# Two batches that share one pass over the weights: turns by quarters of ff in place of halves

## The chip, the cores and the metric

The kernel runs on one core of a Trainium2 chip. The metric is the device time of one execution, in microseconds (us). A core has TensorE (PE, matrix products into the accumulator memory PSUM), VectorE (DVE), ScalarE (ACT), GpSimd (POOL) and SyncE (SP). Each has its own instruction queue, which it works off in order; they wait for each other by semaphores. SP and POOL issue the transfers (DMA) of this kernel.

## The reference

```python
a = exp(phi - phi.max(axis=2)); a = a / (a.sum(axis=2) + 1e-9)   # phi: 8 batches, 8 heads, 576 tokens, 32 slots
k_m = einsum('bhsm,bhsd->bhmd', a, k)                            # k, v, q: 8, 8, 576, 64
v_m = einsum('bhsm,bhsd->bhmd', a, v)
attn = softmax(q @ k_m.T / 8, axis=-1)
x = (attn @ v_m) -> 4608 x 512
h = x @ w_in                                                     # 512 x 2048, float64 in memory
g = maximum(h, 0) ** 2
out = g @ w_out                                                  # 2048 x 512, float64 in memory
```

The weights arrive in float64 and leave as pairs of float32 numbers (a high and a low part); each product is made of three products of such parts.

## The kernel before, in words

**Pairs of batches.** The 8 batches are worked in pairs. One batch is 576 tokens: 512 main rows in four groups of 128, and 64 leftover rows, which are kept until both batches of a pair can put theirs together into one group of 128. The hidden width ff = 2048 is cut into 16 blocks of 128; two blocks make a slice (8 slices).

**A step** (`step(g)`) is one batch and one ff block. `mm1` makes 12 matmuls into two PSUM tiles (tile `h`), ScalarE and VectorE turn them into the high and low part of the squares (tiles `gh`, `glo`, lines 609 to 613; for the leftover rows tile `gl`, lines 610 and 614), and `mm2` makes 12 matmuls that add this block's share of the output into four PSUM accumulators (`acc`, lines 633 to 636). The list `seq` says which batch and block each step is. As long as successive steps belong to one batch, the accumulators go on; where the batch changes, they are evacuated (`evac`) to on-chip memory and the other batch takes them over. `mm2_left` makes the product of the leftover rows of a pair, 48 matmuls into a fifth accumulator that shares the same four places (tile `accl`, line 659).

**The first pair decodes the weights.** `piece(kind, j)` decodes slice j of w_in or w_out in two halves (`decode`, lines 320 to 346): a load of float64 bits into a raw room (SP), six or seven VectorE operations and two ScalarE operations in a work room, and, for w_out after the first slice, a transfer on POOL that adds the work room to the low part (line 343, `wo<-work`). The decoded w_in (tile `wi`, three places) is stored to memory as two float32 parts (POOL, line 346) and read again by `wi_again` (SP, line 351) whenever another batch needs it; the decoded w_out (tiles `wo`) stays on chip. The rooms are tiles that are not yet in use: `free` lists them for each slice, V4 to V7 (later holders of products and of partial sums), the W tiles of later slices, and for slice 7 the tiles of q and of keys and values (`KV`).

**Products with the values.** `memory(b, hh)` makes the attention memory of half of a batch's heads (products `pkv`, line 408, from tiles `KV` and `phi`); `vw_alone` (pair 0) and `vw_step` (later pairs) multiply the slices of w_in by the values' memory, so that the attention's output x is never formed. `attention(b)` makes the attention weights of a batch (tiles `ath`, `atl`; the last subtraction is line 570); its tile q is loaded by line 515.

**Order.** The program lists operations with what they read and write. `Plan.order` lays them on the engines by a list schedule: each operation has a latest start that follows from the due time of its step, `due(g) = (g + 20) * 5200` ns, and from the estimated costs of what comes behind it; of what is ready, an engine takes the operation with the earliest latest start, where preparing operations (`lead`) count 9000 ns earlier. So an operation's place on its engine follows from the position of its step in `seq`. In the first pair `seq` has batch 0 with blocks 0 to 7, batch 1 with 0 to 15, and batch 0 with 8 to 15: 32 steps, numbered 0 to 31. The attention of batch 1 is needed from step 8 on, and slices 4 to 7 at steps 16, 18, 20 and 22.

Of the kernel before, what the change touches and what calls it, by code (L numbers as in the profile page):

```python
# [11 lines left out]
F32 = mybir.dt.float32  # L12
# [7 lines left out]
P = 128  # L20
# [186 lines left out]
def tile_attention_moe(  # L207
# [79 lines left out]
    half = NFF // 2  # L287
    seq = [(b, f) for b, h in ((0, 0), (1, 0), (1, 1), (0, 1)) for f in range(h * half, (h + 1) * half)]
    seq += [(b, f) for b in range(2, B) for f in range(NFF)]
# [292 lines left out]
    def mm1(g):  # L582
# [7 lines left out]
        if ff not in gl or gl[ff][0] != b // 2:  # L590
            gl[ff] = b // 2, st([P, 2, 2 * LEFT], F32R, f"gl{ff}", f"gl{g}")
        G = gl[ff][1]
        lc = slice((b % 2) * LEFT, (b % 2 + 1) * LEFT)
        for h in (0, 1):
# [15 lines left out]
        op({"ACT": act(LEFT)}, lambda e: nc.scalar.activation(G()[:, 0, lc], r()[:, SM:S], AF.Square), [r], [(G, (b % 2, 0))])  # L610
# [3 lines left out]
        vec({"DVE": tt(LEFT)}, lambda e: nc.vector.tensor_sub(G()[:, 1, lc], r()[:, SM:S], G()[:, 0, lc].bitcast(F32)), [r, (G, (b % 2, 0))], [(G, (b % 2, 1))])  # L614
        gt[g] = gh, glo

    def mm2(g):
# [21 lines left out]
        if f1:  # L639
            home = homes(b) if ff == NFF - 1 else None  # L640
            for i in range(NMAIN):
                if ff < NFF - 1:
                    if i % 2 == 0:
                        part[i // 2] = st([P, 2, DM], F32, f"V{4 + i // 2}", f"part{i // 2}")
                    pp = part[i // 2]
                    op({"ACT": act(DM), "DVE": tt(DM)}, lambda e, i=i, a=acc[i], pp=pp: copy(e, pp()[:, i % 2, :], a()), [acc[i]], [(pp, i % 2)])
                else:
                    ot, x = home[i]
                    evac(acc[i], home[i], lambda ot=ot, x=x: ot()[:, x, :], [(b, 4 * i + c) for c in range(4)], b == 0)

    def mm2_left(b, g):
        a = pt("acc", f"accl{b}", 4)
        for ff in range(NFF):
            G = gl[ff][1]
            t = wo[ff]

            def mm(e, ff=ff, G=G, t=t):
                for n, (l, w) in enumerate(((0, 0), (0, 1), (1, 0))):
                    nc.tensor.matmul(a(), G()[:, l, :], t()[:, w],  # L659
                                     start=(ff == 0 and n == 0), stop=(ff == NFF - 1 and n == 2))  # L660

            op({"PE": 690}, mm, [G, (t, 0), (t, 1)], [a], cap=due(g + 2) + 690 * ff, lat=300)
        o = st([P, DM], F32, "o", f"ol{b}")
        evac(a, (o, None), lambda: o(), [(b - 1, 16), (b - 1, 17), (b, 16), (b, 17)])

    def homes(b):

        if b == 0:
            return [(part[i // 2], i % 2) for i in range(NMAIN)]
        tags = ("V6", "V7") if b == 1 else ("vw0", "vw0") if b % 2 == 0 else ("V4", "V5")  # L670
# [3 lines left out]
    def evac(a, home, o, cols, add=False):  # L674
        if add:
            vec({"DVE": tt(DM)}, lambda e: nc.vector.tensor_add(o(), a(), o()), [a, home], [home], port=None)
        else:
            op({"ACT": act(DM), "DVE": tt(DM)}, lambda e: copy(e, o(), a()), [a], [home])
        n = len(cols) // len({x[0] for x in cols})
        for j in range(0, 4, n):  # L680
            b, c = cols[j]

            def store(d, j=j, b=b, c=c):
# [3 lines left out]
            dma(store, 32 * n * DM * 4, [home], [], eng="SP" if b >= B - 2 else "POOL")  # L687


    pos = {x: i for i, x in enumerate(seq)}  # L690

    def step(g):
# [3 lines left out]
        if ff == NFF - 1 and b % 2 == (b > 1):  # L696
            mm2_left(b | 1, g)
# [3 lines left out]
        0: ("V6 V7 W6a", "W6b W7a W7b V4 V5"), 4: ("V6 V7 W5a", "W5b W6a W6b W7a W7b"),  # L701
        5: ("V6 V7", "W6a W6b W7a W7b"), 6: ("V6 V7", "W7a W7b"), 7: ("V6 V7", "q KV"),
# [3 lines left out]
    def piece(kind, j):  # L706
        raws, works = (x.split() for x in free[j if j > 3 else 0])
# [9 lines left out]
    for j in range(4):  # L717
# [9 lines left out]
    for s in range(4):  # L727
        vw_alloc(0, s, (1,))
        for hh in (0, 1):
            wi_again(0, s, hh)  # L730
        vw_alone(s, 1)
        step(8 + 2 * s)
        step(9 + 2 * s)
    for j in range(4, 8):
# [5 lines left out]
        step(8 + 2 * j)  # L740
        step(9 + 2 * j)
    for g in range(24, 32):
        step(g)
# [50 lines left out]
```

## Time and profile before

| | |
|---|---|
| median of 3 runs (all) | 836.11 us (831.14, 836.11, 837.33) |
| span of the profiled execution | 831.4 us; the page gives no time around it |
| TensorE busy | 763.5 us, 92% |
| VectorE busy | 571.2 us, 69% |
| ScalarE busy | 378.1 us, 45% |
| GpSimd busy | 67.4 us, 8% |
| granted TensorE clock, mean | 0.973 |
| moved by transfers | 101.56 MB, mean 122 GB/s |

The profile is one execution. Busy times of an engine are the union of its instructions' times; instructions that are pipelined overlap, so durations of single instructions add up to more than the busy time. The granted clock is a share of full speed: 1.0 is 2.4 GHz, 0.5 is 1.2 GHz, and a value between is a mean over a stretch with both. "Idle before, releaser" is the time in which an engine had nothing running before an instruction, and what let it go on.

### The profile page before, as it was taken

What the parts mean: (1) busy time and instruction counts of PE and PEld (TensorE: products, weight loads), DVE (VectorE), ACT (ScalarE), POOL (GpSimd) and SP (SyncE); (2) the same over time, 40 slices, a digit from 0 to 9 for tenths busy, and PEclk for the clock granted to TensorE, in tenths of its full rate; (3) what the DMA queues carried; (4) which work ended last, traced back from release to release, by engine and by line L of the source; (5) the groups of instructions that cost most, each with busy time, mean ns of one, the idle gap of its engine ahead of it and who ended that gap; (6) DMA issues with size and microseconds to landing.
All of it is one profiled execution on the core that took longest, in us unless ns stands there. A gap on an engine that the chain in (4) does not pass through costs nothing.

```text
span 831.4 us, 12939 instructions
## 1 busy us (share of the span) xinstructions
PE 763.5 (92%) x4756; PEld 643.3 (77%) x4756; DVE 571.2 (69%) x1266; ACT 378.1 (45%) x871; POOL 67.4 (8%) x105
## 2 busy tenths in 40 slices
PE   3468789989989899999999999999999999999995
PEld 2245578878768688888888888888788888888884
DVE  3899899898446756696768465786768556774540
ACT  1235466656535245563436355463435355552320
POOL 3113112222100100001000100000000100000000
PEclk9959999999999899999999999999999999999998
DMA  7947966657665443322552533323422433100001
GB/s 210 302 153 223 261 192 203 178 174 212 159 161 151 116 132 102 102 80 52 143 142 72 135 111 99 117 54 81 140 61 69 138 93 99 53 16 36 1 1 63
DMA packets 93091, 101.56 MB, mean 122 GB/s; under 512 B 24868, under 2 KB 78116, under 8 KB 93028
## 3 DMA queue, kind: packets, MB, share of 16 engines
q1 hardware_dynamic: 80292, 81.55, 33.2%
q0 software_dynamic: 12736, 19.19, 9.5%
q8 instruction: 37, 0.61, 0.3%
q14 instruction: 26, 0.21, 0.1%
HBM read 79.17 MB, written 17.83 MB: 117 GB/s over the span
## 4 chain that ended last, share of the span: by engine, by line
PE 73%; issue 10%; DVE 8%; DMA 3%; ACT 2%; POOL 2%; SPq 0%; POOLq 0%; DVEq 0%; ACTq 0%
PE h L603 20%; PE acc L636 12%; PE acc L633 12%; PE acc L634 12%; PE accl L659 4%; PE pvw L494 4%; PE psc L532 3%; PE pkv L408 3%; DMA q<-in_q_dram 2%; PE pvw L475 1%; DVE vw L503 1%; DVE qT L527 1%; ACT vw L260 1%; DMA wo<-work 1%; DVE work L325 1%
## 5 line engine op out<-in xcount | busy, mean ns | idle before, releaser
L603 PE MATMUL h<-ath,vw 128*128 128x320 f32 (+1 forms) x1024 | 213.9, 300 | 8.9 <-ACT ath L260 6.3
L633 PE MATMUL acc<-wo,gh 128*128 128x512 f32 x512 | 207.0, 404 | 2.7 <-ACT gh L609 2.5
L634 PE MATMUL acc<-wo,gh 128*128 128x512 f32 x512 | 201.7, 394 | 0.0
L603 PEld LDWEIGHTS h<-ath,vw 128*128 128x128 f32 x1024 | 172.5, 190 | 25.7 <-ACT ath L260 6.7
L636 PE MATMUL acc<-wo,glo 128*128 128x512 f32 x512 | 161.5, 409 | 3.0 <-DVE glo L613 2.8
L503 DVE TENSOR_TENSOR vw<-pvw,vw 64x256 fp32r<-64x256 f32 x192 | 78.5, 420 | 68.0 <-ACT vw L260 66.2
L633 PEld LDWEIGHTS acc<-wo,gh 128*128 128x128 f32 x512 | 97.1, 190 | 23.3 <-ACT gh L609 3.8
L260 ACT CAST vw<-pvw 64x256 fp32r<-64x256 f32 (+1 forms) x206 | 74.9, 381 | 83.9 <-PE pvw L494 37.6
L603 PE MATMUL h<-atl,vw 128*128 128x256 f32 (+1 forms) x512 | 110.5, 297 | 0.0
L634 PEld LDWEIGHTS acc<-wo,gh 128*128 128x128 f32 x512 | 96.9, 189 | 16.9
L636 PEld LDWEIGHTS acc<-wo,glo 128*128 128x128 f32 x512 | 90.5, 191 | 21.4 <-DVE glo L613 7.6
L609 ACT ACTIVATE gh<-r 128x512 fp32r<-128x512 f32 x128 | 80.7, 631 | 45.3 <-DVE r L608 38.5
L613 DVE TENSOR_TENSOR glo<-r,gh 128x512 fp32r<-128x512 f32 x128 | 87.6, 684 | 5.1 <-ACT r L611 2.9
L608 DVE TENSOR_SCALAR r<-h 128x256 f32<-128x256 f32 (+1 forms) x109 | 49.7, 458 | 59.0 <-PE h L603 58.1
L607 ACT ACTIVATE r<-h 128x256 f32<-128x256 f32 (+1 forms) x147 | 58.8, 407 | 67.8 <-PE h L603 59.8
L603 PEld LDWEIGHTS h<-atl,vw 128*128 128x128 f32 x512 | 83.0, 190 | 0.5 <-DVE atl L570 0.2
L611 ACT ACTIVATE r<-r 128x576 f32<-128x576 f32 x93 | 63.7, 685 | 2.1
L610 ACT ACTIVATE gl<-r 128x64 fp32r<-128x64 f32 x128 | 32.7, 256 | 63.2 <-DVE r L608 61.0
L659 PE MATMUL accl<-wo,gl 128*128 128x512 f32 x192 | 53.0, 400 | 0.1
L532 PE MATMUL psc<-qT,kb 128*128 128x256 f32 (+1 forms) x128 | 43.3, 465 | 5.8 <-DVE S L536 3.1
L494 PE MATMUL pvw<-wi,VTh 128*128 128x256 f32 x192 | 38.1, 290 | 3.8 <-DVE vw L503 3.7
L659 PEld LDWEIGHTS accl<-wo,gl 128*128 128x128 f32 x192 | 35.4, 191 | 7.3 <-DVE o L260 0.5
(94 smaller groups left out, 818.5 us busy)
## 6 DMA issues: line engine op xcount, KB each, us to landing
wi<-w_in_hi SPq DMA_DIRECT2D x56, 256.0 KB
wi<-w_in_lo SPq DMA_DIRECT2D x56, 256.0 KB
q<-in_q_dram SPq DMA_DIRECT2D x32, 288.0 KB
KV<-in_k_dram SPq DMA_DIRECT2D x32, 256.0 KB
KV<-in_v_dram SPq DMA_DIRECT2D x32, 256.0 KB
raw<-in_moe_w_in_dram SPq DMA_DIRECT2D x16, 512.0 KB
raw<-in_moe_w_out_dram SPq DMA_DIRECT2D x16, 512.0 KB
out_dram<-o POOLq DMA_DIRECT2D x20, 256.0 KB, 8.4
```

Source lines behind the costliest of these rows:

```text
L260: nc.scalar.copy(o, i) if e == "ACT" else ENG[e].tensor_copy(o, i)
L494: nc.tensor.matmul(pw()[:, x * SL:(x + 1) * SL], l()[:, 2 * hh + x, :], w(r, x), start=(i == 0), stop=(i == 2))
L503: vec({"DVE": tt(SL)}, lambda e, V=V, pr=pr, src=src: nc.vector.tensor_sub(V()[pr, 1, hh, :], src(), V()[pr, 0, hh, :].bitcast(F32)), [pw, ...
L532: nc.tensor.matmul(pq()[:, 0:32 * n], kb()[:, x].rearrange("p h m -> p (h m)"), qT()[:, x, 0:n].rearrange("p c t -> p (c t)"), start=(x == ...
L603: nc.tensor.matmul(p()[:, 0:n], V()[:, l, hh, c0:c0 + P], x()[:, hh, cs], start=(i == 0), stop=(i == 5))
L609: op({"ACT": act(SM)}, lambda e: nc.scalar.activation(gh(), r()[:, 0:SM], AF.Square), [r], [gh])
L611: op({"ACT": act(S), **({} if b < 2 else {"DVE": tt(S)})}, lambda e: nc.scalar.activation(r(), r(), AF.Square) if e == "ACT" else nc.vecto ...
L613: vec({"DVE": tt(SM)}, lambda e: nc.vector.tensor_sub(glo(), r()[:, 0:SM], gh().bitcast(F32)), [r, gh], [glo])
L633: nc.tensor.matmul(a(), gh()[:, c], t()[:, 0], start=f0, stop=False)
L634: nc.tensor.matmul(a(), gh()[:, c], t()[:, 1], start=False, stop=False)
L636: nc.tensor.matmul(a(), glo()[:, c], t()[:, 0], start=False, stop=f1)
L659: nc.tensor.matmul(a(), G()[:, l, :], t()[:, w], start=(ff == 0 and n == 0), stop=(ff == NFF - 1 and n == 2))
```

## The change

The first pair's turns become quarters of ff, and neighbouring turns of one batch are joined: batch 0 with blocks 0 to 3, batch 1 with 0 to 7, batch 0 with 4 to 11, batch 1 with 8 to 15, batch 0 with 12 to 15. Every time a batch hands the accumulators over, its sums go to its four places on chip (V4, V5 for batch 0; V6, V7 for batch 1): the first time as a copy, later by an addition that only VectorE may do; the last time they are stored too. The leftover rows' squares are kept by quarters (four tiles `gl0` to `gl3`, of which the first pair uses two), and their product is made in four parts as soon as both batches have a quarter. The decoder's rooms and the tiles of the products move accordingly.

```diff
+    turns = [(b, range(4 * x, 4 * x + 4)) for x in range(4) for b in ((0, 1) if x % 2 == 0 else (1, 0))]
+    turns += [(b, range(NFF)) for b in range(2, B)]
+    joined = [turns[0]]
+    for b, fs in turns[1:]:
+        if b == joined[-1][0]:
+            joined[-1] = b, range(joined[-1][1].start, fs.stop)
+        else:
+            joined.append((b, fs))
+    seq = [(b, f) for b, fs in joined for f in fs]
...
-            later = 0 if n == 0 and s > 3 else 1
+            later = 1 if n or s // 2 % 2 == 0 else 0
...
-        ts_ = [wi[0, s, bp if s < 4 else 0, hh] for hh in (0, 1)]
+        ts_ = [wi[0, s, bp if s < 2 else 0, hh] for hh in (0, 1)]
...
+            new = b not in part
+            if new:
+                part[b] = homes(b)
             for i in range(NMAIN):
...
+                ot, x = part[b][i]
+                o = lambda ot=ot, x=x: ot()[:, x, :]
+                evac(acc[i], (ot, x), o, not new)
+                if ff == NFF - 1:
+                    store((ot, x), o, [(b, 4 * i + c) for c in range(4)])
...
-    def mm2_left(b, g):
+    def mm2_left(b, g, fs):
...
+        last = {}
+        for x in (b - b % 2, b - b % 2 + 1):
+            last[x] = max((f for bb, f in seq[:g + 1] if bb == x), default=-1) + 1
+        stop = min(last.values())
+        start = done.get(b // 2, 0)
+        if stop > start:
+            mm2_left(b | 1, g, range(start, stop))
+            done[b // 2] = stop
...
-        0: ("V6 V7 W6a", "W6b W7a W7b V4 V5"), 4: ("V6 V7 W5a", "W5b W6a W6b W7a W7b"),
-        5: ("V6 V7", "W6a W6b W7a W7b"), 6: ("V6 V7", "W7a W7b"), 7: ("V6 V7", "q KV"),
+        0: ("V6 V7 W6a", "W6b W7a W7b V4 V5"), 2: ("V6 V7 W6a", "W6b W7a W7b"), 4: ("W6a W7a W5a", "W6b W7b W5b"),
+        5: ("W6a W7a gl2", "W6b W7b gl3"), 6: ("W7a gl2", "W7b gl3"), 7: ("gl2 KV", "gl3 q"),
...
-    for j in range(4):
+    for j in (0, 1):
         piece("wi", j)
         vw_alloc(0, j, (0,))
         vw_alone(j, 0)
...
-    for s in range(4):
-        vw_alloc(0, s, (1,))
...
-    for j in range(4, 8):
+    g = 4
+    for j in range(NSL):
+        if j < 2:
+            vw_alloc(0, j, (1,))
+            for hh in (0, 1):
+                wi_again(0, j, hh)
+            vw_alone(j, 1)
+            for _ in (0, 1):
+                step(g)
+                g += 1
+            continue
         piece("wi", j)
         vw_alloc(0, j)
         for bp in (0, 1):
             vw_alone(j, bp)
         piece("wo", j)
...
```

In `free` the first list of a slice are the raw rooms and the second the work rooms. `memory(1, ...)` and `attention(1)` stand ahead of the second loop in both kernels; before, four slices stand ahead of them, after, two. `mm2_left` takes the blocks of one part as `fs`, evacuates the first part by a copy and the later ones by additions. `wi_again` runs for four slices of the first pair before and for two after.

## Rows read from the trace of the kernel before

**Rows 1.** The page's picture of the span in 40 slices: TensorE busy, TensorE clock, tenths.

```profile
PE   3468789989989899999999999999999999999995
PEclk9959999999999899999999999999999999999998
```

**Rows 2.** Stages: length, busy us of PE, PEld, DVE, ACT, POOL; clock, transfer share, GB/s.

```profile
62.00:97.00 35.00, 27.39 (x191) 20.95 (x191) 31.18 (x72) 15.90 (x36) 8.01 (x11) 0.90 0.86 241
97.00:125.00 28.00, 23.29 (x124) 18.70 (x124) 27.90 (x64) 16.77 (x38) 4.72 (x6) 1.00 0.69 204
125.00:208.00 83.00, 78.53 (x473) 69.82 (x471) 72.96 (x146) 51.31 (x111) 19.04 (x24) 1.00 0.66 192
208.00:270.00 62.00, 57.54 (x435) 46.33 (x433) 33.87 (x79) 29.32 (x70) 3.61 (x8) 0.97 0.61 158
270.00:291.00 21.00, 17.57 (x74) 14.54 (x74) 16.06 (x35) 5.44 (x14) 2.68 (x4) 0.84 0.46 115
291.00:420.00 129.00, 128.85 (x827) 111.19 (x826) 90.39 (x205) 64.90 (x154) 4.64 (x9) 1.00 0.36 100
```

**Rows 3.** Order of time of VectorE, 62 to 290 us: start, length, line, operation.

```profile
70.78 0.68 DVE L339 TENSOR_TENSOR wo<-work,wo 128x512 fp32r<-128x512 f32 x1
104.38 0.69 DVE L613 TENSOR_TENSOR glo<-r,gh 128x512 fp32r<-128x512 f32 x1
112.87 0.68 DVE L339 TENSOR_TENSOR wo<-work,wo 128x512 fp32r<-128x512 f32 x1
124.08 0.49 DVE L570 TENSOR_TENSOR atl<-at,ath 128x320 fp32r<-128x320 f32 x1
125.42 0.69 DVE L613 TENSOR_TENSOR glo<-r,gh 128x512 fp32r<-128x512 f32 x1
201.67 0.68 DVE L339 TENSOR_TENSOR wo<-work,wo 128x512 fp32r<-128x512 f32 x1
266.65 0.69 DVE L613 TENSOR_TENSOR glo<-r,gh 128x512 fp32r<-128x512 f32 x1
281.66 0.71 DVE L527 STREAM_TRANSPOSE qT<-q 128x512 f32<-128x512 f32 x1 [3.33 <-DMA q<-in_q_dram]
```

**Rows 4.** Groups of VectorE, 125 to 208 us: count, busy us, mean ns, idle before.

```profile
L327 DVE SCALAR_TENSOR_TENSOR work<-raw,work 128x512 f32<-128x512 uint32 x16 | 10.9, 684 | 0.1
L324 DVE TENSOR_SCALAR work<-raw 128x512 uint32<-128x512 uint32 x15 | 6.5, 432 | 0.0
L322 DVE TENSOR_SCALAR work<-raw 128x512 f32<-128x512 f32 x13 | 5.5, 422 | 4.9 <-DMA wo<-work 3.1 <-DMA raw<-in_moe_w_in_dram 1.6 <-DMA raw<-in_moe_w_out_dram 0.2
```

**Rows 5.** Instructions on the tile part: count, ns least/median/most, first and last start.

```profile
L676 DVE TENSOR_TENSOR part<-acc,part x4: 668/682/692, 270.5 to 285.5; 128x512 f32<-128x512 f32 x4
L260 ACT COPY part<-acc x3: 582/587/592, 128.1 to 130.2; 128x512 f32<-128x512 f32 x3
L260 DVE COPY part<-acc x1: 682/682/682, 130.5 to 130.5; 128x512 f32<-128x512 f32 x1
```

**Rows 6.** Order of time of TensorE where batch 1 hands over to batch 0.

```profile
224.04 0.63 PE L636 MATMUL acc<-wo,glo 128*128 128x512 f32 x2
226.16 0.39 PE L633 MATMUL acc<-wo,gh 128*128 128x512 f32 x1
```

**Rows 7.** Transfers issued from 0 to 210 us: line, count, size.

```profile
wi<-w_in_hi SPq DMA_DIRECT2D x11, 256.0 KB
```

**Rows 8.** Order of time of TensorE before batch 2's first product.

```profile
214.93 1.43 PE L408 MATMUL pkv<-KV,phi 128*32 128x128 f32 x38
254.87 1.43 PE L408 MATMUL pkv<-KV,phi 128*32 128x128 f32 x40
286.99 0.63 PE L603 MATMUL h<-ath,vw 128*128 128x256 f32 x2
```

**Rows 9.** Order of time of the queues of POOL and SP after slice 7.

```profile
202.65 0.85 POOL L343 DMA_DIRECT2D wo<-work  x1 [4.84 <-DVE wo L339]
203.03 0.37 SPq L359 DMA_DIRECT2D KV<-in_k_dram  x1
```

More of the change, by code (lines that the diff above doesn't have):

```diff
@@ L639, in mm2 @@
         if f1:
-            home = homes(b) if ff == NFF - 1 else None
+            new = b not in part
+            if new:
+                part[b] = homes(b)
             for i in range(NMAIN):
[L642 to L649, printed above, removed]
-    def mm2_left(b, g):
-        a = pt("acc", f"accl{b}", 4)
-        for ff in range(NFF):
-            G = gl[ff][1]
+                ot, x = part[b][i]
[4 more added lines that the diff above has]
+    def mm2_left(b, g, fs):
+        a = pt("acc", f"accl{b}_{fs.start}", 4)
+        for ff in fs:
+            G = gl[b // 2, ff // 4]
             t = wo[ff]
@@ L658, in mm, with evac @@
                 for n, (l, w) in enumerate(((0, 0), (0, 1), (1, 0))):
[L659 to L664, printed above, removed]
+                    nc.tensor.matmul(a(), G()[:, ff % 4, l, :], t()[:, w],
+                                     start=(ff == fs.start and n == 0), stop=(ff == fs.stop - 1 and n == 2))
+            op({"PE": 690}, mm, [(G, (ff % 4, x, l)) for x in (0, 1) for l in (0, 1)] + [(t, 0), (t, 1)], [a], cap=due(g + 2) + 690 * ff, lat=300)
+        if fs.start == 0:
+            part["left"] = st([P, DM], F32, "o", f"ol{b}")
+        o = part["left"]
+        evac(a, (o, None), lambda: o(), fs.start > 0)
+        if fs.stop == NFF:
+            store((o, None), lambda: o(), [(b - 1, 16), (b - 1, 17), (b, 16), (b, 17)])
     def homes(b):
-        if b == 0:
-            return [(part[i // 2], i % 2) for i in range(NMAIN)]
-        tags = ("V6", "V7") if b == 1 else ("vw0", "vw0") if b % 2 == 0 else ("V4", "V5")
+        tags = ("V4", "V5") if b == 0 else ("V6", "V7") if b == 1 else ("vw0", "vw0") if b % 2 == 0 else ("V4", "V5")
         t = [st([P, 2, DM], F32, x, f"o{b}_{i}", 2 if x == "vw0" else 1) for i, x in enumerate(tags)]
         return [(t[i // 2], i % 2) for i in range(NMAIN)]
-    def evac(a, home, o, cols, add=False):
+    def evac(a, home, o, add):
         if add:
@@ L681, in evac, with st_ @@
             b, c = cols[j]
-            def store(d, j=j, b=b, c=c):
+            def st_(d, j=j, b=b, c=c):
                 rows = out[b * S:(b + 1) * S, :].rearrange("(p c) e -> c p e", c=NC)
                 d(rows[c:c + n], o()[32 * j:32 * (j + n), :])
-            dma(store, 32 * n * DM * 4, [home], [], eng="SP" if b >= B - 2 else "POOL")
+            dma(st_, 32 * n * DM * 4, [home], [], eng="SP" if b >= B - 2 else "POOL")
     pos = {x: i for i, x in enumerate(seq)}
+    done = {}
     def step(g):
@@ L706, in piece @@
     def piece(kind, j):
-        raws, works = (x.split() for x in free[j if j > 3 else 0])
+        raws, works = (x.split() for x in free[max(x for x in free if x <= j)])
         for h in (0, 1):
@@ L739, in tile_attention_moe @@
         piece("wo", j)
[L740 to L743, printed above, removed]
+        for _ in (0, 1):
+            step(g)
+            g += 1
+        if j % 2:
+            for _ in range(4):
+                step(g)
+                g += 1
     for n in range(1, NPAIR):
```

25 lines of the change are left out of this document (10 added, 15 removed).

## The prediction

> **What bounds the kernel now.** I read the page's picture of the span first, then the busy time of each engine by stage, then VectorE's order of time in the opening, then the way in which the second pair of batches starts.
>
> The picture [rows 1] shows TensorE busy in nine tenths of nearly every slice from 125 us on, and not before; its clock line has its lows in the same opening and once more near 280 us. The stages [rows 2] give sizes. From 62 to 97 us TensorE is idle for 35.00 - 27.39 = 7.6 us, from 97 to 125 for 4.7, from 125 to 208 for 4.5, from 208 to 270 for 4.5 and from 270 to 291 for 3.4: together 24.7 us. After 291 us it idles 0.15 us in 129, so nothing there can be won by order. What holds TensorE in the opening is VectorE: 31.18 of 35 us and 27.90 of 28 us busy. From 125 to 208 VectorE is still at 88%, and from 208 to 270 at 55%: the bound passes to TensorE at about 125 us.
>
> VectorE's order of time [rows 3] says what the opening waits for. The weights of slices 0 and 1 (each slice is 256 columns of ff, two steps) are decoded at 70.78 + 0.68 = 71.5 us. The fourth step's subtraction is at 104.38, slice 3 is decoded at 113.6, the attention of batch 1 ends at 124.6, and the eighth step's subtraction is at 125.42. From there the 24 further steps of the pair take until 266.65: 141.2 / 24 = 5.9 us a step. So up to 125 us a step waits for the decoder, and batch 1, which needs no new weights for its first eight steps, cannot help, because its attention is only finished when the first eight steps are done.
>
> **The change part by part.** All sums are against the profiled execution, of which the page gives the span, 831.4 us, and no time around it. The runs are 831.14, 836.11 and 837.33 us: the span lies 4.7 us under their median and 0.3 over the lowest. I take differences from the trace and put them on the median.
>
> *The order of steps.* Steps 0 to 3 stay batch 0, 4 to 11 become batch 1, 12 to 19 batch 0, 20 to 27 batch 1, 28 to 31 batch 0. Due times follow the position, so the attention of batch 1 is due four steps earlier, slices 2 and 3 four steps later, slices 4 and 5 as before, slices 6 and 7 four steps later (26 in place of 22 for slice 7). What VectorE has to do before step 4 is now: both attentions and two slices, in place of one attention, three slices. Price of a slice: a half of w_in takes three VectorE operations of the short kind and four of the long one, a half of w_out (slices after the first) three and three, so a slice is 12 x 0.43 + 14 x 0.68 = 14.7 us by durations [rows 4], and by start distances, which are 0.08 us shorter each, 12.6. Between 71.5 and 125 us VectorE did two slices (25.2), eight subtractions (4.8), three products' splits (1.8), the idle 35 - 31.18 + 0.1 = 3.9 us at most, and, for the beginning of slice 4 and the small parts, some 4 us more by estimate; what is left, about 14 us, was attention of batch 1. If that 14 us comes first, behind four subtractions (2.4), four splits (2.4) and the same waits, it ends at 71.5 + 14 + 4.8 + 3.9 = 94 us, in place of 124.6. From 94 us TensorE has eight steps without new weights; at 5.9 us each the eighth subtraction falls at 94 + 4 x 5.9 = 117.6 in place of 125.42. Slice 2 is then due at step 8 and ready at 94 + 12.6 + 3 = 110, slice 3 at step 10 (129 us) and ready at 126: in time, barely. Gain 7.8 us. Its bounds: 12.3 us, all idle time of 62 to 125, and -5.9, one step lost because attention now comes ahead of slice 1. I take **7**, the nearest whole value, since the order of steps is what these rows show.
>
> *From 125 to 208 us* slices 6 and 7 are due four steps later, so TensorE should wait less for them. Idle there is 4.5 us; bounds 0 and 4.5, taken **2**, the middle.
>
> *Evacuations.* Four accumulators change owner five times in place of three, and the left product ends four times in place of once: 13 evacuations become 24, and all 11 more are additions, which only VectorE may do, at 0.68 us [rows 5]: 7.5 us of VectorE. Today's copies go three to ScalarE and one to VectorE. Where they change owner at step 23 TensorE ends the old step at 224.04 + 0.63 and starts the new at 226.16, with the next products of the first layer between [rows 6]: no wait. Four additions in a row need 2.7 us of VectorE alone, where the cover is one step's first product, so two more changes may cost 0 to 2 x 2.7 us; I take **-1**, nearer to the row that shows no wait. The left products themselves are the same 48 matmuls a pair: nothing. The additions lie where VectorE is 55 to 88% busy; if that cover were gone they would cost their 7.5 us (a rival, below).
>
> *Queues.* On SP the re-reads of w_in for batch 1 fall from 16 to 8 transfers of 256 KB in the first pair; the row counts 11 of each half up to 210 us, of which 8 are this pair's [rows 7]. That is 2.1 MB less, at the 204 GB/s of 97 to 125 us 10 us of the transfers' time, in a stage where TensorE does not wait for them: no gain counted. On POOL the stores of w_in and the adding transfers of w_out keep their number and order; batch 1's stores move four steps later and stand behind the last adding transfers, so nothing waits for them. The decoder's work rooms fall from five to three for slices 2 to 4, its raw rooms stay three; VectorE lost 3.1 us to an adding transfer with five and four rooms [rows 4], so I set 0 to 5 us of VectorE waits, hidden up to step 8's reserve; none counted.
>
> *Where it can be given back.* Batch 2's first product starts at 286.99 [rows 8]. It stands behind the keys and values of batches 2 and 3, whose first load waits for slice 7's last adding transfer: issued at 202.65, load at 203.03 [rows 9], and then products of memory at 214.93, ..., 254.87: 13.3 us each, paced by loads. From load to first product are 84 us. After the change, slice 7 ends about 2 us later by VectorE's count: seven of the eleven additions fall ahead of it (4.8 us), less some of the 4.9 us of waits [rows 4]. The 32 us from 254.87 to 286.99 can shrink: VectorE is 55% busy there and waits 3.33 us for q [rows 3]. I estimate 9 us of shrinking, so 287 + 2 - 9 = 280. TensorE's side gives 287 - 7 - 2 + 1 = 279. The later of both holds: batch 2 starts at 280, **7 us earlier**, and from there the kernel is TensorE's and unchanged. 836.1 - 7 = **829**.
>
> **The rivals.**
> *All of it is kept (822).* Idle of 62 to 125 falls from 12.3 to 3, of 125 to 208 from 4.5 to 1.5, and the start of batch 2 loses 2.9 of its 7.9 us, since loads that are asked for earlier meet fewer re-reads: 9.3 + 3 + 2.9 - 1 = 14 us. For it: transfers are 86% busy in 62 to 97, and 2.1 MB of them go. Against: the 13.3 us rounds.
> *The 84 us stand (838).* The opening gains 7 us, or the planner leaves the order of engines nearly as it was, and batch 2 still waits 84 us for the load, which comes 2 us later: +2. For it: those rounds. Against: 32 us of the chain are not loads.
> *Slice 7 slides (851).* It is due four steps later and holds two rooms of keys and of q until its last adding transfer. Placed by its due time at today's pace it ends 23.5 us later; the load is at 226.5, and with the shortened 75 us batch 2 starts at 301.5, 14.5 us late. It decides from a load at 220.4 on, where the start passes 295.4. For it: VectorE serves what is due first. Against: VectorE has idle time, and the same rooms are due to batch 2 as well.
> *VectorE is the bound throughout (844).* Then 11 additions cost their 7.5 us. Rows speak against it: VectorE is full to 125 us alone, and at most two of the eleven fall there. The Trainium skill, Perfetto Trace Analysis, section Identifying the Most-Contended Engine, names the engine with the highest occupancy as the one to relieve first; by that the opening would be VectorE's, and a change that gives it more work would lose. The trace agrees for the opening and not for the stages in which the additions lie.
>
> **How the numbers follow.** The forecast has 0.42 (own range 824 to 834), all kept 0.28, the 84 us 0.13, the slide 0.10, VectorE 0.07. A measurement of this kernel can tell about 1%, 8.4 us, from no change: under 827.7 or over 844.5. Faster: 0.27 of all kept and 0.06 of the forecast, 0.33. Slower: the slide, 0.10, and 0.04 of the upper ends of the others, 0.14. The rest, 0.53, is within. The range reaches from 818, beyond all kept, to 844, at VectorE's; outside lie the slide and the far end of all kept, under 0.2.
>
> **What would show it.** The attention of batch 1 ending near 94 us and the eighth subtraction near 118 show the first step right; an end past 110 shows it wrong. Idle of TensorE from 62 to 125 should be about 5 us. The last adding transfer of slice 7 near 205 and batch 2's first product near 280 show the handing over right; a load after 220 is the slide. TensorE waiting for additions at steps 12, 20 and 28 would show my -1 too small. A VectorE that is full after 125 us would prove the last rival.

## The result and the profile after

| | before | after |
|---|---|---|
| median | 834.63 us (4 runs, 831.14 to 837.33) | 824.41 us (4 runs, 821.78 to 826.54) |
| ratio after / before, 95% interval | | 0.9879 [0.9839, 0.9919] |
| profiled execution: span | 831.4 us | 823.8 us (its time 825.51) |
| TensorE, VectorE busy | 763.5, 571.2 us | 762.6, 576.0 us |
| moved by transfers | 101.56 MB | 99.46 MB |

The change makes the kernel 10.2 us faster, 1.2%. In the profiled executions the span is 7.6 us shorter; TensorE's busy time differs by 0.9 us, so 6.7 us of it are idle time that is gone. The question of this section is where.

The page's picture of the changed kernel, in 40 slices, for [rows 1]:

```profile
PE   3358889999999999999999999999999999999995
PEclk9977989999999999999999999999999999999998
```

The low places that the kernel before has from 166 to 291 us (single 8s in the busy line, an 8 in the clock line near 280 us) are gone. The opening, the first five or six digits, looks no better. The stages of the changed kernel say it in numbers (length, busy us of PE, PEld, DVE, ACT, POOL, then clock, transfer share, GB/s), for [rows 2]:

```profile
62.00:97.00 35.00, 29.22 (x192) 22.14 (x193) 26.91 (x60) 14.93 (x35) 4.94 (x7) 0.83 0.73 223
97.00:125.00 28.00, 24.07 (x119) 19.77 (x118) 24.73 (x55) 16.22 (x37) 5.04 (x6) 0.88 0.43 127
125.00:208.00 83.00, 81.46 (x473) 71.44 (x472) 80.39 (x165) 54.98 (x117) 21.29 (x26) 1.00 0.64 181
208.00:270.00 62.00, 59.15 (x449) 47.96 (x448) 45.05 (x103) 26.37 (x64) 6.84 (x12) 1.00 0.68 185
270.00:291.00 21.00, 21.00 (x117) 18.13 (x116) 19.40 (x43) 13.33 (x34) 4.01 (x6) 1.00 0.56 134
291.00:420.00 129.00, 128.84 (x867) 111.12 (x866) 91.45 (x205) 65.85 (x156) 3.29 (x7) 1.00 0.38 106
```

Length less busy time of TensorE, against [rows 2]: 62 to 97 us 5.8 (before 7.6), 97 to 125 us 3.9 (4.7), 125 to 208 us 1.5 (4.5), 208 to 270 us 2.9 (4.5), 270 to 291 us 0.0 (3.4). Before 62 us the changed kernel idles 3.4 us more than the kernel before, so the whole opening, 0 to 125 us, went from 44.4 to 45.2: nothing was won there. From 125 to 291 us idle time fell from 12.4 to 4.4, by 8.0 us; after 291 us it rose by 0.5. The three together are the 6.7 us.

The clock's lows in this stretch are gone too. The granted clock is 1.00 in all three stages from 125 us on, where the kernel before had 1.00, 0.97 and 0.84: there it was 0.50, which is 1.2 GHz, from 243.6 to 246.8 us, after TensorE had waited 3.00 us until 242.00, and again from 288 to 291 us, after a wait of 3.43 us until 285.57. What the slower clock cost by itself is not separated here.

VectorE's order of time of the changed kernel (start, length, line, operation, in brackets the idle time before it and what ended it), for [rows 3]; lines have moved, L621 is the subtraction `glo`, L345 the last operation of a half slice, L576 the last of an attention:

```profile
82.47 0.68 DVE L621 TENSOR_TENSOR glo<-r,gh 128x512 fp32r<-128x512 f32 x1
94.69 0.52 DVE L542 STREAM_TRANSPOSE S<-psc 128x320 f32<-128x320 f32 x1 [3.71 <-PE psc L538]
107.75 0.49 DVE L576 TENSOR_TENSOR atl<-at,ath 128x320 fp32r<-128x320 f32 x1
134.62 0.68 DVE L621 TENSOR_TENSOR glo<-r,gh 128x512 fp32r<-128x512 f32 x1
218.62 0.69 DVE L345 TENSOR_TENSOR wo<-work,wo 128x512 fp32r<-128x512 f32 x1
280.33 0.65 DVE L621 TENSOR_TENSOR glo<-r,gh 128x512 fp32r<-128x512 f32 x1
```

The attention of batch 1 does move ahead, from 124.6 to 108.2 us, but by 16 us and not by 30; the eighth subtraction falls at 134.62, 9 us later than before. VectorE, full before (59.1 us busy of 63 from 62 to 125 us), now idles 11.4 of them: 3.71 us of it in one piece behind TensorE's scores. Two more pauses of 2.4 us each stand behind TensorE's products for `vw` and for the memory. An attention is a chain that goes to and fro between TensorE, VectorE and ScalarE, and with the decoder's slices placed after it VectorE has less to fill its pauses with. Slice 7 ends at 218.62 + 0.69 in place of 202.4 us, and the pair's last subtraction falls at 280.33 in place of 266.65: the first pair now runs further into the stretch in which the second is made ready.

Batch 2's keys and values and its first product, TensorE's order of time in the changed kernel, for [rows 8]:

```profile
209.28 1.43 PE L414 MATMUL pkv<-KV,phi 128*32 128x128 f32 x38
246.07 1.54 PE L414 MATMUL pkv<-KV,phi 128*32 128x128 f32 x40 [0.25 <-DMA KV<-in_v_dram]
282.07 0.40 PE L611 MATMUL h<-ath,vw 128*128 128x256 f32 x2
```

And the two queues, POOL's and SP's, in the changed kernel, for [rows 9]:

```profile
213.81 0.91 POOL L349 DMA_DIRECT2D wo<-work  x1 [1.51 <-DVE wo L345]
219.60 0.84 POOL L349 DMA_DIRECT2D wo<-work  x1 [4.88 <-DMA KV<-in_v_dram]
...
203.50 0.37 SPq L365 DMA_DIRECT2D KV<-in_k_dram  x1
218.86 1.14 SPq L521 DMA_DIRECT2D q<-in_q_dram  x2
```

In the kernel before, SP waited 7.6 us for an adding transfer until it could issue the load at 203.03. That was not the last one, which was issued at 202.65, only 0.38 us ahead, but the one before it:

```profile
196.89 0.92 POOL L343 DMA_DIRECT2D wo<-work  x1 [0.82 <-DVE gl L614]
SPq L359 <- DMA wo<-work: 7.6, 1, 7.6
```

By the semaphores in the trace this transfer, issued at 196.89, landed at 202.90 and let the load of keys go; the last one landed at 207.41 and let the load of q go at 207.54. In the changed kernel the last two adding transfers slid to 213.81 and 219.60 us, the load of keys only to 203.50: it no longer stands behind either, but behind VectorE's last read of the room (L333). The load of q at 218.86 still stands behind an adding transfer, the one of 213.81. Products of memory run 6 to 9 us earlier, and batch 2 starts at 282.07 in place of 286.99.

In the decoder, VectorE's groups of the changed kernel from 125 to 208 us (count, busy us, mean ns, idle before) answer to [rows 4]:

```profile
L333 DVE SCALAR_TENSOR_TENSOR work<-raw,work 128x512 f32<-128x512 uint32 x19 | 12.9, 680 | 0.0
L328 DVE TENSOR_SCALAR work<-raw 128x512 f32<-128x512 f32 x17 | 7.6, 446 | 1.2 <-DMA wo<-work 1.2
```

VectorE waits 1.2 us there for work rooms in place of 3.1, no longer waits for raw loads (1.8 us before), and is busy for 80.39 us of 83 in place of 72.96. The evacuations, for [rows 5] (the tile is now called `o`; instructions on it by VectorE from 100 to 300 us, ns least/median/most, first and last start):

```profile
L685 DVE TENSOR_TENSOR o<-acc,o x12: 645/691/692, 204.6 to 286.1; 128x512 f32<-128x512 f32 x12
L260 DVE COPY o<-acc x2: 676/678/679, 155.0 to 155.6; 128x512 f32<-128x512 f32 x2
```

TensorE's waits from 125 to 291 us in the changed kernel (us, times, longest):

```profile
PE psc L538 <- DVE rz_None L555: 1.6, 1, 1.6
PE h L611 <- ACT r L615: 1.3, 1, 1.3
PE pvt L451 <- DVE vx L447: 1.0, 2, 0.8
PE accl L666 <- DVE o L685: 0.5, 1, 0.5
PE accl L666 <- DVE o L260: 0.5, 1, 0.5
PE pvw L481 <- DVE vw L489: 0.4, 1, 0.4
PE pkv L414 <- DMA KV<-in_v_dram: 0.2, 1, 0.2
```

Before, the longest in the same view were the splits `vw` (VectorE late) and the keys and values:

```profile
PE pvw L494 <- DVE vw L503: 3.4, 1, 3.4
PE pkv L408 <- DMA KV<-in_v_dram: 3.0, 1, 3.0
PE pvw L475 <- DVE vw L483: 2.5, 2, 2.2
```

These 8.9 us are now 0.6. That is about the gain; the experiments ask what took them away.

### The profile page after: what moved, and what is told of

The parts are those of the page before. It is cut to its first block, busy times and chain, and to the rows that moved or that the text cites. A ratio compares the mean times of both kernels' runs of the same rounds, so it can differ in the third digit from the quotient of the medians.

```text
span 823.8 us, 12916 instructions
## 1 busy us (share of the span) xinstructions
PE 762.6 (93%) x4756; PEld 643.3 (78%) x4756; DVE 576.0 (70%) x1276; ACT 378.3 (46%) x872; POOL 67.8 (8%) x105
## 2 busy tenths in 40 slices
DMA packets 90915, 99.46 MB, mean 121 GB/s; under 512 B 24740, under 2 KB 75940, under 8 KB 90852
## 4 chain that ended last, share of the span: by engine, by line
PE 74%; DVE 9%; issue 8%; ACT 3%; DMA 3%; POOL 1%; SPq 0%; POOLq 0%; DVEq 0%; ACTq 0%
PE h L611 20%; PE acc L641 13%; PE acc L642 12%; PE acc L644 12%; PE accl L666 5%; PE pvw L500 4%; PE psc L538 3%; PE pkv L414 3%; DMA phi<-in_phi_dram 1%; PE pvw L481 1%; DMA q<-in_q_dram 1%; ACT vw L260 1%; DVE glo L621 1%; DVE work L331 1%; DVE work L333 1%
## 5 line engine op out<-in xcount | busy, mean ns | idle before, releaser
L509 DVE TENSOR_TENSOR vw<-pvw,vw 64x256 fp32r<-64x256 f32 x192 | 78.6, 420 | 63.9 <-ACT vw L260 62.0
L615 ACT ACTIVATE r<-h 128x320 f32<-128x320 f32 (+1 forms) x148 | 59.4, 407 | 85.5 <-PE h L611 79.3
L616 DVE TENSOR_SCALAR r<-h 128x320 f32<-128x320 f32 (+1 forms) x108 | 49.2, 457 | 59.7 <-PE h L611 59.0
L621 DVE TENSOR_TENSOR glo<-r,gh 128x512 fp32r<-128x512 f32 x128 | 87.4, 683 | 4.9 <-ACT r L619 3.1
L538 PE MATMUL psc<-qT,kb 128*128 128x256 f32 (+1 forms) x128 | 41.4, 448 | 5.4 <-DVE S L542 1.8
L696 POOL DMA_DIRECT2D out_dram<-o x24 | 16.2, 678 | 298.0 <-ACT o L260 200.8
```

The lines of the kernel that those rows point to most:

```text
L509: vec({"DVE": tt(SL)}, lambda e, V=V, pr=pr, src=src: nc.vector.tensor_sub(V()[pr, 1, hh, :], src(), V()[pr, 0, hh, :].bitcast(F32)), [pw, ...
L538: nc.tensor.matmul(pq()[:, 0:32 * n], kb()[:, x].rearrange("p h m -> p (h m)"), qT()[:, x, 0:n].rearrange("p c t -> p (c t)"), start=(x == ...
L615: op({"ACT": act(n) - 30, **({} if b < 2 else {"DVE": tt(n)})}, lambda e, cs=cs, n=n, p=p: nc.scalar.activation(r()[:, cs], p()[:, 0:n], A ...
L621: vec({"DVE": tt(SM)}, lambda e: nc.vector.tensor_sub(glo(), r()[:, 0:SM], gh().bitcast(F32)), [r, gh], [glo])
```

## The experiments

Each ran beside the kernel before, on the same chip, and a ratio is to the kernel before on that chip; the differences in us between changed kernels are taken from the ratios or the medians as they stand. One caution holds for all of them: the planner lays out the whole kernel anew for every edit, so each variant differs from the kernel it is made from by its edit and by its order of work; only e7, e9 and e12 share one order on TensorE, VectorE, ScalarE and POOL. First the places where the prediction saw a rival, then the parts of the change one by one, then the order itself.

### e1: the room of keys and values as a work room

In the changed kernel `KV` is a raw room of slice 7, which is free after its last read (L333). Before, it was a work room, which stays occupied until the adding transfer that reads it has landed.

```diff
-        7: ("gl2 KV", "gl3 q"),
+        7: ("gl2 gl3", "q KV"),
```

> The changed kernel, but slice 7 is decoded with keys and values' tiles and q as work rooms, as before the change, in place of raw rooms; the two freed leftover tiles become its raw rooms. Nothing else differs. Room theory: batch 2's keys and values come early after the change because a raw room is free at its last read, a work room only when the adding transfer has landed; undone, the first product of memory of batch 2 moves from 204-210 us to about 215, TensorE idles some 5 us more between 208 and 291 us, and the time is 829 us. Order theory (the saving comes from the order of steps, which leaves TensorE steps of the first pair beside batch 2's preparation): 824 to 826 us, idle from 125 to 291 us stays near 4.4 us.

Measured: 841.32 us (6 runs, 840.5 to 842.51), ratio 1.0084 [1.005, 1.0117], 17 us slower than the changed kernel. Its order of time, POOL's and SP's queue:

```profile
205.99 0.90 POOL L349 DMA_DIRECT2D wo<-work  x1 [4.67 <-DVE gl L622]
...
209.40 0.38 SPq L365 DMA_DIRECT2D KV<-in_k_dram  x1
```

and TensorE's waits from 125 to 291 us, the two longest:

```profile
PE psc L538 <- DVE qT L533: 7.6, 1, 7.6
PE pvw L481 <- ACT wi L260: 3.9, 1, 3.9
```

The load is issued again behind the landing of an adding transfer, that of 205.99, 6 us later than in the changed kernel; it isn't the last one, which follows at 216.74. SP stands for it in one piece:

```profile
SPq L365 <- DMA wo<-work: 17.2, 1, 17.2
```

The keys' first load, which the changed kernel issues at 183.23, stands behind this wait too and comes at 210.94. So the room's part in the load's delay is shown. Its price isn't: of 11.8 us more idle time from 125 to 291 us, 5.4 lie before 208 us, where the products of these keys have hardly begun, and the longest wait, 7.6 us of batch 2's scores, is for a q that is loaded at 273.16, long after the adding transfers; there the order of work has changed. That quarters can't do without the raw room is likely, since 1.0084 lies outside all the orders with it (0.9876 to 0.9993, below), but not shown apart from the order.

### e2: the same room edit in the kernel before

```diff
-        7: ("V6 V7", "q KV"),
+        7: ("V6 KV", "q V7"),
```

> The kernel before with one exchange of rooms for slice 7: keys and values' tile as raw room, V7 as work room. Room theory: the loads for batch 2 start 8 us earlier, the waits of 3.0 us for keys and values and 3.4 us behind the load of q near 240 and 285 us go, 829 us. Order theory: within 2 us of the kernel before, 833 to 836 us.

Measured: 833.27 us (12 runs), ratio 0.9989 [0.9959, 1.0018]. The load comes at 198.42 in place of 203.03, and in the profiled execution TensorE idles 7.2 us from 125 to 291 us in place of 12.4, but that execution (830.08 us) lies 3.2 us under this kernel's median. In halves the room that the load waits for gives nothing that can be measured.

### e3: the leftover rows' product in two parts in the kernel before

```diff
-            mm2_left(b | 1, g)
+            mm2_left(b | 1, g, range(0 if b else half, NFF))
...
+        if ff == NFF - 1 and b == 1:
+            mm2_left(1, g, range(half))
```

> The kernel before, halves as before, with the leftover rows' product of the first pair made in two parts, after step 23 and after step 31, one addition more. Theory that the parts of the left product made the saving (TensorE has its work earlier and no long product at the change of pairs): 829 to 831 us, idle from 208 to 291 us down from 7.9 to about 4 us. Order theory: 833 to 836 us; the part taken from the end uncovers waits there, idle from 270 to 291 us up by up to 3 us.

Measured: 834.14 us (12 runs), ratio 1.0013 [0.9987, 1.0038]. Nothing.

### e5: both rooms of the next pair raw

```diff
-        7: ("gl2 KV", "gl3 q"),
+        7: ("KV q", "gl2 gl3"),
```

> The changed kernel, slice 7 with keys and values' tile and q's tile both as raw rooms and the two leftover tiles as work rooms (in the changed kernel q is a work room). Room theory: q too is free at its last read, so the first q of batch 2 is loaded some 10 us earlier than 218.9 us; since the start of batch 2 hangs on the keys and values and not on the first q, no more than 0 to 3 us come of it: 821 to 825 us. Theory that any exchange of rooms merely shuffles the planner's order: a difference either way of 5 us and more.

Measured: 827.89 us (6 runs), ratio 0.9925 [0.9897, 0.9952]: no better than the changed kernel. The loads of q were issued no earlier (225 us against 218.86).

### e8: the additions doubled

Each of the additions of the evacuations is made by two VectorE operations (a subtraction, and 2a minus it, the same sum): 15 operations of 0.68 us more, 10.2 us.

```diff
-            vec(..., lambda e: nc.vector.tensor_add(o(), a(), o()), ...)
+            vec(..., lambda e: nc.vector.tensor_sub(o(), a(), o()), ...)
+            vec(..., lambda e: nc.vector.scalar_tensor_tensor(o(), a(), 2.0, o(), ALU.mult, ALU.subtract), ...)
```

> The changed kernel with every addition at a handing over made by two VectorE operations on the accumulator in place of one (o = a - o, then o = 2 a - o), 15 operations of 0.68 us more in the first pair, the sums unchanged up to rounding. Forecast's step (evacuations lie beside other work, about 0.1 us each): 824 to 827 us. Rival that VectorE is the bound: 10 us more, 834 us.

Measured: 824.22 us (6 runs), ratio 0.9876 [0.9848, 0.9904]. Nothing is lost that can be measured. But the planner has moved work in return: VectorE has 8 operations more and not 15, since a net 7 others now go to ScalarE, and it is busy 6.0 us longer, not 10.2; the order is another one too. So this run shows that the kernel can take the doubled additions, and not what they would cost in an unchanged order.

### e6 and e11: the attention of batch 1 with no lead, and with half

A preparing operation counts 9000 ns earlier in the planner. In e6 the attention of batch 1 and its memory get 0, in e11 4500.

```diff
+    plan.pull = 0            # e11: LEAD // 2
     memory(1, 0)
     memory(1, 1)
     attention(1)
+    plan.pull = LEAD
```

> The changed kernel; memory and attention of batch 1 lose the 9000 ns by which preparing operations are preferred, nothing else is changed. Latency theory of the opening (VectorE stood idle for 11.4 us from 62 to 125 us because attention's serial chain was put ahead of the decoder): the first step's subtraction comes back from 82.5 towards 73 us, VectorE's idle time from 0 to 125 us falls by 5 to 10 us, and the time is 818 to 823 us. Work theory of the prediction (VectorE is full, only the sum of work counts): the eighth step's subtraction stays near 134 us and the time at 824 to 826 us.

> The changed kernel with the attention of batch 1 given half of the planner's lead (4,500 ns in place of 9,000). Without a lead it took 825.0, the same as with it. If the place of this attention in the opening is worth nothing between those two ends: 824.5 (822 to 828). If there is an optimum between, with VectorE neither idle behind the attention's chain nor the attention late: 820 (816 to 822), and TensorE's idle time from 0 to 125 us below 42.

Measured: e6 825.0 us (6 runs), ratio 0.9897 [0.9857, 0.9937]; e11 829.36 us (6 runs), ratio 0.9914 [0.9884, 0.9944]. In e6 the first four subtractions come 12 to 16 us earlier than in the changed kernel (the first at 70.69, the fourth at 87.40), the attention ends at 111.3, and VectorE idles 12.0 us less up to 125 us; TensorE idles 42.7 us there, 2.5 less. The time is the same. No optimum shows at half the lead. Where the attention stands in the opening moves idle time about and hardly removes it.

### e4 and e7: the transfers that fell away, put back

e4 lets batch 1 read slices 2 and 3 again, as before the change (8 transfers of 256 KB). e7 leaves that as changed and adds 8 transfers of the same size from the stored parts of w_in to a spare place in chip memory; nothing reads them.

```diff
# e4
-        ts_ = [wi[0, s, bp if s < 2 else 0, hh] for hh in (0, 1)]
+        ts_ = [wi[0, s, bp if s < 4 else 0, hh] for hh in (0, 1)]
...
+            if bp and j < 4:
+                for hh in (0, 1):
+                    wi_again(0, j, hh)
# e7
+            if bp and j < 4:
+                for hh in (0, 1):
+                    spare_copy(j, hh, due(g))
```

> The changed kernel with the re-reads of slices 2 and 3 for batch 1 put back: 8 more transfers of 256 KB, the same values. Theory that 2.1 MB fewer re-reads made the saving: 829 to 833 us, waits for re-read weights near 105 to 125 us. Order theory: 824 to 826 us; the transfers' share from 97 to 125 us rises from 0.43 to about 0.6 without a wait on TensorE's chain.

> The changed kernel with 8 more transfers of 256 KB, issued on SP where the re-reads of slices 2 and 3 stood: they copy the stored w_in parts to an unused place in memory and take no place on the chip, so nothing waits for them. Traffic theory of the 8.6 us that the kept re-reads cost: 830 to 833 us. Place theory (the re-reads take two of the three places of decoded w_in and hold up the next slice): 824 to 826 us.

Measured: e4 832.98 us (12 runs), ratio 0.9987 [0.9963, 1.0011]; e7 833.08 us (12 runs), ratio 0.9987 [0.9961, 1.0012]. Both lose the whole gain. Taken alone they say that the transfers that fell away carry it, and SP's queue offers a reason: these are waits of SP in e7 (us, times, longest), with raw loads standing behind them:

```profile
SPq L367 <- DMA w_in_hi<-wi: 11.0, 2, 7.0
SPq L367 <- DMA w_in_spare<-w_in_hi: 8.5, 3, 3.1
```

That reading is what e9, e10 and e12 test, and it falls.

### e9: the spare transfers without a wait

As e7, but the spare transfers read the kernel's own input w_in, so none waits for a store. TensorE, VectorE, ScalarE and POOL have the instructions of e7 in the order of e7.

```diff
-            dma(lambda d, i=i: d(rows(spare), rows(w_in_parts[i])), ...)
+            dma(lambda d, i=i: d(rows(spare), rows(lambda: w_in.bitcast(U32))), ...)
```

> The changed kernel with the same 8 extra transfers of 256 KB from chip memory to chip memory as in the run before with spare transfers, but read from the kernel's own input w_in in place of the stored parts, so that none of them waits for a store. The instructions of TensorE, VectorE, ScalarE and POOL stand in the same order as there; only SP's queue differs, whose transfers start without a wait. Theory A, that what costs is SP's queue standing still (11.0 and 8.5 us behind waits for w_in stores, with raw loads and KV loads behind them): the time falls back to 824 (822 to 827), and no wait of SP of the spare transfers is over 2 us. Theory B, that what costs is the added traffic of 2 x 2.1 MB, whenever it runs: 833 (830 to 836), with the idle time of TensorE in 125 to 208 us still near 6. In between, 827 to 830: both have a part.

Measured: 834.0 us (12 runs), ratio 0.9974 [0.9948, 0.9999]. These waits of SP are gone, the time is not back. Theory A, SP's queue, falls.

### e10: the re-reads that are left on POOL's queue

```diff
-                dma(lambda d, x=x: ..., lead=True)
+                dma(lambda d, x=x: ..., eng="POOL" if n == 0 else "SP", lead=True)
```

> The changed kernel with the 8 re-reads that are left (slices 0 and 1, for batch 1) issued from POOL's queue in place of SP's, so that their waits for the stores of w_in no longer hold up raw loads on SP. Theory A, that waits in order on SP's queue are what costs: 822 or less (817 to 823), with TensorE's idle time from 0 to 125 us below 43 (45.2 in the changed kernel). Theory B, that traffic is what costs: no change, 824 (822 to 827). A third way: POOL's waits hold its adding transfers and stores back, and the time is 826 to 832.

Measured: 829.89 us (6 runs), ratio 0.9918 [0.9889, 0.9948]; TensorE idles 47.0 us to 125 us in place of 45.2. This is the third way, or no difference by the ratios' intervals; nothing is won.

### e12: planned, but not moved

As e9, but the spare transfers are only reckoned with by the planner; they are never issued. The instructions of TensorE, VectorE, ScalarE and POOL and their order are those of e9 and e7; the bytes are those of the changed kernel.

```diff
-            dma(lambda d, i=i: d(rows(spare), ...), 2048 * P, r=..., w=...)
+            dma(lambda d: None, 2048 * P, r=..., w=...)
```

> The same as the run before (spare transfers that read the input and wait for no store), but the 8 spare transfers are only reckoned with when the order of work is planned and are not issued: TensorE, VectorE, ScalarE, POOL do the same instructions in the same order as there, and 2.1 MB less are moved in each direction. Theory B, that the traffic costs (the time was the same with and without waits on SP's queue): the time falls by 8 us, ratio to the kernel before 0.988 as the changed kernel has it, and TensorE's idle time in 125 to 208 us falls from 5.5 to 2 or below. Theory C, that the order costs into which the planner puts the other work when it reckons with these transfers: the ratio stays at 0.997 to 0.999, with the idle time at 5 to 6. Both: 0.991 to 0.995.

Measured: 833.79 us (12 runs), ratio 0.9993 [0.9967, 1.0019]. Theory B, the traffic, falls as well: 2.1 MB more in each direction and a standing queue (e7), the traffic without the wait (e9) and neither (e12) give 0.9987, 0.9974 and 0.9993. What costs 9 us is the plan (theory C): e12 does the work of the changed kernel, with its transfers, its rooms and its steps, in another order on the engines and on SP's and POOL's queues. The plan also says who does what: ten casts and rectifications that VectorE has in the changed kernel go to ScalarE in e12 and three operations the other way, so VectorE has 1269 operations in place of 1276.

The stages of e12 show where (columns as above):

```profile
125.00:208.00 83.00, 77.29 (x445) 67.95 (x443) 75.68 (x156) 53.35 (x113) 21.17 (x26) 0.98 0.62 175
208.00:270.00 62.00, 58.23 (x436) 47.59 (x434) 40.39 (x87) 27.58 (x64) 6.82 (x12) 0.97 0.68 172
270.00:291.00 21.00, 18.97 (x96) 16.37 (x97) 17.84 (x44) 10.09 (x27) 0.00 (x0) 0.92 0.36 107
```

TensorE idles 5.7, 3.8 and 2.0 us there, as the kernel before does (4.5, 4.5, 3.4) and the changed kernel does not (1.5, 2.9, 0.0). Over the whole span it idles 4.7 us more than in the changed kernel and is busy 3.4 us longer (766.0 us against 762.6), which make the 8.1 us between the spans; why it is busy longer stays open, for the mean granted clock is no lower (0.986 against 0.980). VectorE has as much to do and from 125 to 208 us gets less done, 75.68 us of 83 in place of 80.39. Its waits in that stage of e12, the longest:

```profile
DVE work L328 <- DMA wo<-work: 4.2, 3, 2.4
```

One of them can be followed in the order of time, VectorE's rows and then TensorE's:

```profile
164.42 0.43 DVE L328 TENSOR_SCALAR work<-raw 128x512 f32<-128x512 f32 x1 [2.40 <-DMA wo<-work]
...
167.24 0.69 DVE L499 TENSOR_TENSOR vw<-pvw,vw 128x512 fp32r<-128x512 f32 x1
```

```profile
168.07 1.19 PE L491 MATMUL pvw<-wi,VTh 128*128 128x256 f32 x4 [2.78 <-DVE vw L499]
```

The first operation of a half slice stands in VectorE's queue while its work room is still being read by an adding transfer. VectorE, which works off its queue in order, stands for 2.40 us; the split `vw` that stands behind it comes late, and TensorE waits 2.78 us for it. Right behind, from 167.6 to 170.8 us, the granted clock is 0.50 (1.2 GHz). In the changed kernel the order has put this operation where the room is nearly free: 1.2 us of such waits.

All kernels together, with TensorE's idle time in the profiled execution (length less busy time) and VectorE's waits for adding transfers from 125 to 208 us. The last three columns are of one execution each, which lies up to 3.4 us from the median of its kernel (e6, e11):

| kernel | ratio | idle 0 to 125 us | idle 125 to 291 us | VectorE behind adding transfers |
|---|---|---|---|---|
| e8 additions doubled | 0.9876 | 44.0 | 3.1 | 1.6 |
| the changed kernel | 0.9879 | 45.2 | 4.4 | 1.2 |
| e6 no lead | 0.9897 | 42.7 | 5.4 | 1.0 |
| e11 half lead | 0.9914 | 43.6 | 6.7 | 3.5 |
| e10 POOL's queue | 0.9918 | 47.0 | 6.2 | 1.6 |
| e5 both rooms raw | 0.9925 | 42.2 | 9.1 | 4.9 |
| e9 no wait | 0.9974 | 42.4 | 9.9 | 3.8 |
| e4 re-reads kept | 0.9987 | 43.4 | 9.1 | 4.4 |
| e7 spare transfers | 0.9987 | 42.4 | 11.9 | 4.4 |
| e2 halves, raw room | 0.9989 | 42.8 | 7.2 | 4.4 |
| e12 planned alone | 0.9993 | 43.2 | 11.5 | 4.2 |
| the kernel before | 1 | 44.4 | 12.4 | 3.1 |
| e3 halves, left in two | 1.0013 | 43.6 | 10.1 | 3.0 |
| e1 work room | 1.0084 | 43.8 | 16.2 | 0 (raw loads 2.6) |

The ratio follows the fourth column and not the third: over the 14 rows the correlation with the idle time from 125 to 291 us is 0.92, with that of the opening -0.24. The last column is 1.0 to 1.6 us in the three fastest kernels and 3.0 or more in the slower half, e1 aside; but e5, with 4.9 us in the faster half, and e1 show that other waits count as much, so it is one of the ways and not the only one. That this particular wait by itself costs the 9 us was not tried.

## Why the prediction was right, and where it was not

The time, 824.4 against 829 (818 to 844), and the sign came out. That is luck in part: the range is wide enough to hold a kernel that gains nothing (834.6), and the sum behind it did not come out: its largest term failed, and two that were set small or at nothing hold what happened.

- **The order of steps, 7 us: wrong.** The step that failed is "if that 14 us comes first": it took the attention of batch 1 for 14 us of VectorE's work that could be done in one piece. Its end came at 108.2 us, 14 us later than the 94 worked out, and with "an end past 110" as the mark for wrong it is near that mark; the eighth subtraction, at 134.62, is past everything that was foreseen. From 62 to 125 us TensorE idled 9.7 us where 5 were foreseen (12.3 before), and 3.4 us more before 62 us. VectorE idled 11.4 us of 63, mostly behind the attention's to and fro, and the opening's idle time rose by 0.8 us. e6, which puts the decoder first again, gets the steps earlier and the same time. The bound below, -5.9 us, was the right kind of end; the measured value lies between.
- **From 125 to 208 us, 2 us: right, mis-sized.** 3.0 us (4.5 to 1.5).
- **Evacuations, -1 us: right.** In the changed kernel TensorE waits twice for 0.5 us at `accl`, once behind an addition and once behind a copy; no wait shows at an accumulator of the main rows. That speaks against the rival that VectorE is the bound throughout (844), and e8, which doubles the additions, loses nothing, if in another order. The Trainium skill, Perfetto Trace Analysis, section Identifying the Most-Contended Engine, names the fullest engine as the one to relieve first; no run here relieves VectorE from 125 to 208 us, where it is 97% busy in the changed kernel, and e8's doubled additions start only at 199 us, so the rule is not tested in that stage.
- **Queues, no gain counted: right**, against what e4 and e7 first seemed to say. e9 and e12 differ by the 2.1 MB and SP's queue alone, with ratios 0.9974 and 0.9993. What e4 loses was not taken apart further; its order is another one too. The work rooms, five to three for some slices, show no cost either: VectorE's waits for adding transfers fell from 3.1 to 1.2 us. That they could fall, and what it would be worth, was not foreseen.
- **Giving back: the start of batch 2 nearly right, for a wrong reason.** Forecast 280, measured 282.07. Slice 7 was to end 2 us later; its last adding transfer slid by 17 us. That is most of the slide (851), whose premise came true and whose price did not. The prediction has the new `free` list before it and says of the rooms only that slice 7 "holds two rooms of keys and of q until its last adding transfer"; that holds for a work room, and `KV` had become a raw room. It also took the wrong transfer for the releaser: the load at 203.03 waited for the adding transfer of 196.89, and the last one, of 202.65, held q. With `KV` as a work room the load does stand behind an adding transfer, and the time is 841.3 (e1), in another order. The chain from the load to batch 2's first product took 78.6 us, 75 were estimated. Batch 2 starts 4.9 us earlier and the span is 7.6 us shorter, so "from there the kernel is TensorE's and unchanged" missed 2.7 us.

So the gain is 8.0 us of TensorE's stalls from 125 to 291 us: 3.0 to 208 us, and 5.0 where the second pair is made ready (208 to 291 us), a stage in which the prediction looked for what is given back. **Shown:** the idle time of this stretch goes with the ratio (all 14 kernels); the traffic and SP's queue don't matter at a given order (e7, e9, e12, within intervals of 0.0025 to either side); neither side edit does it in the old order of steps (e2, e3); the load of keys goes free of the adding transfers by the raw room (the changed kernel against e1); and the same work with the same transfers loses it all in another plan (e12). **Argued only:** that the gain needs the raw room, and that the additions cost nothing, since e1 and e8 have other orders; and that it is above all the decoder's first operation behind its room that makes the difference: e12's rows show the chain once, its share of the 9 us was not measured. **Open:** how much of the gain belongs to quarters as such. The planner has made eight orders for quarters with the raw room here (e7, e9 and e12 share one); they lie between 0.9876 and 0.9993, and the three of halves between 0.9989 and 1.0013. Quarters seem to be the better side, by about 0.8% on the mean of the eight, 0.992, but the scatter of the orders is as large as that, and few orders of halves were tried. No variant beats the changed kernel by more than the intervals.

## What to carry to other kernels

Where a planner writes the order of the queues, an experiment that adds or removes work also draws another order: before a cost is put on the traffic, the queue or the added work, run the same plan with the work planned and not issued (e12), or the finding may be the planner's. Read the gain from the stage in which TensorE idles and check that variants which win and lose differ in that stage. When a change moves a buffer to another role, look up which last reader sets it free: in the changed kernel the raw room `KV` was loaded anew at 203.50 and the work room q at 218.86, 15 us apart.

## What the runs showed that had not been expected

Another plan for the same work, from the same planner with 8 transfers more to reckon with, changed the time by 9 us (824.4 to 833.8), more than 2.1 MB of extra transfers (e9 against e12, -0.0019 in the ratio) or a queue of SP that stands for 19.5 us (e7 against e12, -0.0006). Moving the attention of batch 1 ahead by 16 us gave VectorE 11.4 us of idle time in a stretch that it had filled before, for no gain in TensorE's idle time of the opening, which stayed between 42 and 47 us in all 14 kernels.
